# The first 512 rows of expert 0 moved into the attention, weight loads moved among the dispatches, and half tiles as two sums side by side

## The chip, the cores and the metric

The kernel runs on one core of a Trainium2 chip. The metric is the device time of one execution in microseconds (us); the kernel before takes 458.68 us (median of 6 runs, 457.5 to 460.51). A core has TensorE (matmuls, PE in the profile, its weight loads PEld), VectorE (DVE), ScalarE (ACT), GpSimd (POOL) and SyncE (SP). Each takes its instructions in order and waits on semaphores; transfers are issued from queues of GpSimd (software DMA), SyncE and ScalarE and run on 16 shared DMA engines.

## What is computed

A linear attention with phi(x) = elu(x) + 1, and on its result a mixture of experts with a noisy top-2 router:

```python
q_p, k_p = phi(q), phi(k)                       # (8 batches, 8 heads, 576, 64)
kv  = einsum('bhsd,bhse->bhde', k_p, v)
z   = sum(k_p, axis=2)
x   = einsum('bhsd,bhde->bhse', q_p, kv) / (einsum('bhsd,bhd->bhs', q_p, z)[..., None] + 1e-6)
x   = x.transpose(0, 2, 1, 3).reshape(4608, 512)

noisy = x @ w_gate + log1p(exp(x @ w_noise)) * noise      # 8 experts
top2  = the two largest of a row; top2_w = their softmax
for e in range(8):
    rows = the rows that have e among their two
    out[rows] += top2_w[rows, e] * (relu(x[rows] @ w1[e]) @ w2[e])   # w1 512x1024, w2 1024x512
```

## The kernel before

**Attention.** The 8 batches go in 4 groups of two. For each group: `load` brings q, k, v (GpSimd queue, cast to bf16), `exp` (ScalarE) and `phi` (VectorE) make phi(k) and phi(q), `kv_mm` multiplies phi(k) by v, `kv_ev` masks the result into `kvbd` (VectorE), `kv_b1` and `kv_b2` append the router's weights, already multiplied by kv, `qt` transposes phi(q), and `num` (three steps t per group; part 0 on TensorE, part 1 on VectorE) gives x (in `xr`, one of two buffers by turns) and the router's logits. `attention()` writes the order of all engines out by hand: group n's q and k are prepared beside group g = n - 1's `num` and routing.

**Routing.** Per unit (`UNITS`: groups 0, 1, 2 whole, group 3 in two parts) `rt_a` makes logits and noise scale, `rt_b` the top two and, with matmuls against a triangle of ones, each row's rank within its expert; `rt_c` adds the running count `carry` and so gets each row's position. `dispatch` scatters rows of x with an indirect DMA per column and choice into the DRAM table `x_sorted` (18 for a whole group, 72 in all), a short memset between two of them. Every row appears twice: as a first visit (kind F, the lower-numbered of its two experts) and a second (kind S). `ROUNDS` holds bounds: after the unit named, `carry` of experts 0, 1, 2 is raised to at least this row, so that rows below the bound are complete and may be read while later dispatches run.

**Experts.** A block is up to four tiles of 128 rows of one expert. `xn_load` brings its rows (SyncE queue), `meta_load` gates and indices, `xn_t` transposes on TensorE with a copy on ScalarE, `mm1` is relu(x @ w1) in eight parts (TensorE, then ScalarE), `mm2` is the product with w2 per tile, eight matmuls of 128x128 by 512 into one PSUM bank, then y = gate * sum on VectorE. First visits are put into the DRAM table `part` (SyncE). Second visits gather their first part (`gather`, GpSimd) into L, add it and scatter y to the output (`put`, GpSimd). Between F and S an expert has a mixed tile kind M: rows fetched by an indirect DMA (`mid_gather`, tile xm), two tiles, the second half full (64 rows). Experts 0 and 7 end with a half tile too. So there are eight half tiles: one of expert 0, one each of experts 1 to 6, one of expert 7, which is the last of all.

`interval(cur, prev, weights, nxt)` interleaves on TensorE: `mm1` of the current block, two parts at a time, with one `mm2` tile of the block before, and the transposes of the next block after the second and third of these. The gather of the next block and weight loads follow.

**The seam.** `routing()` runs after the attention: block a0 (expert 0, F tiles 0 to 3) with the ranks of units 3 and 4 between its parts, then a1 (expert 1, F 0 to 2), b0 (expert 0, F 4 and 5), b1 (expert 1, F 3 and 4), a2 (expert 2, F 0 to 3), c0 (expert 0, F 6 to 9, the last one half full). `xn_load(b0)`, b1 and a2 need the dispatches of unit 2; c0 needs all. `w_load(e, i)` is one of four weight pieces of an expert (512 KB in bf16): those of experts 0 and 1 stand among the dispatches of units 1 and 2, those of 2 and 3 after the last dispatch.

GpSimd's order from 64.8 us on, as the time line has it: 12 dispatches of unit 0, a q load, 6 more, unit 1 with four pieces, unit 2 with four pieces, unit 3 (12), unit 4 (6), the last dispatch written at 181.16, eight weight pieces, gathers of xm.

Lines named later: 261 `num`, 378 the memset between dispatches, 387 `dispatch`, 431 and 435 `w_load`, 443 `meta_load`, 498 `mid_gather`, 560 and 563 `xn_load`, 586 and 590 `xn_t`, 607 `gather`, 624 and 626 `mm1`, 635 to 641 `mm2`, 649 and 655 `put`. In the kernel after, the same code stands 1 to 34 lines lower.

Of the kernel before, what the change touches and what calls it, by code (L numbers as in the profile page):

```python
# [15 lines left out]
P = 128  # L16
# [17 lines left out]
ROUNDS = [(1, (512, 384, 256)), (2, (768, 640, 512))]  # L34
# [15 lines left out]
def build_constants(tc, consts, w_gate, w_noise, noise):  # L50
# [23 lines left out]
    c["gap"], c["gap2"] = tile_("gap", [P, 192]), tile_("gap2", [P, 352])  # L74
# [48 lines left out]
class PhaseA:  # L123
# [252 lines left out]
    def apart(self):  # L376

        self.nc.gpsimd.memset(self.c["gap"][:], 0.0)  # L378
# [22 lines left out]
class PhaseB:  # L401


    def __init__(self, ctx, tc, w1, w2, x_sorted, part, out):
# [5 lines left out]
        self.yp = [pool("B_y", 4)]  # L410
# [4 lines left out]
        self.left, self.ready = [], set()  # L415
# [212 lines left out]
    def mm2(self, b, t):  # L628
# [5 lines left out]
        for fc in range(8):  # L634
            nc.tensor.matmul(out=ps[0:m], lhsT=b["hT"][:, fc, t * P : t * P + m], rhs=w2[:, fc, :],  # L635
                             start=(fc == 0), stop=(fc == 7))
# [3 lines left out]
        else:  # L640
            nc.vector.tensor_scalar(out=y[0:m], in0=ps[0:m], scalar1=gate, scalar2=None, op0=ALU.mult)

    def put(self, b, t):
# [9 lines left out]
        if kind != "F":  # L653
# [6 lines left out]
            tc.add_to_no_dep_group("osc", r.ins)  # L660
            nc.gpsimd.memset(self.c["gap2"][:], 0.0)
# [82 lines left out]
def attention(pa, pb, c, x_sorted, zrow):  # L744
# [30 lines left out]
    first = pb.block(0, ("F", 0, 4))  # L775
    for g in range(3):
# [7 lines left out]
        if g == 1:  # L784
            pa.dispatch(0, 6, 9)
# [8 lines left out]
        pa.phi(n, "q", 0, 1)  # L794
        pa.num(g, 2, 1)
        pa.phi(n, "q", 2)
        if g == 0:
            pa.load(3, "k")
        pa.rt_a(g)
        pa.kv_ev(n, 0)  # L800
        pa.kv_ev(n, 1)
        pa.kv_b1(n)
        pa.qt(n, 0)
# [4 lines left out]
        if g == 0:  # L808
            pa.dispatch(0, 0, 6)
        else:  # L810
            pb.w_tiles(g - 1)
            for i in range(4):
                pa.dispatch(g, 2 * i, 2 * i + 2)
                pb.w_load(g - 1, i)
            pa.dispatch(g, 8, 9)
        if g == 1:
            pb.xn_load(first, 0)
            pb.meta_load(0, "F", 0, 4, 0)
            pb.meta_load(1, "F", 0, 3, 0)
# [4 lines left out]
    pa.num(3, 0, 1)  # L824
    pa.num(3, 1, 0)
# [4 lines left out]
    return first  # L830


def routing(pa, pb, c, first):

    pb.left += [0] * 6 + [1] * 5 + [2] * 4
# [3 lines left out]
    pb.xn_load(a1, 0)  # L839
    pb.meta_load(0, "F", 4, 2, 1)  # L840
    pb.xn_load(b0, 1)
    pb.meta_load(1, "F", 3, 2, 1)
    pb.xn_load(b1, 1)
    pb.meta_load(2, "F", 0, 4, 1)
    pb.xn_load(a2, 1)
    pb.xn_t(a0, 0)
    pb.xn_t(a0, 1)
    pb.mm1(a0, 0)
    pa.rt_b(3)
    pb.mm1(a0, 1, 2)  # L850
    pa.rt_c(3)
    pa.dispatch(3)
    pa.rt_a(4)
# [142 lines left out]
```

## Time and profile before

| what | value |
|---|---|
| median of 6 runs | 458.68 us |
| profiled execution | 460.76 us |
| its span, first to last instruction | 458.9 us |
| TensorE busy | 365.5 us (80%) |
| GpSimd busy | 286.9 us (63%) |
| ScalarE, VectorE busy | 192.9 us (42%), 179.2 us (39%) |
| mean granted TensorE clock | 0.903 |
| first dispatch, last dispatch (GpSimd) | 64.8 us, 181.16 us |
| last matmul ends, last scatter written, end | 449.8 us, 451.8 us, 458.9 us |

The profile is of one execution. Its lines of slices cut the span into 40 parts of 11.5 us; a digit is the busy share of an engine in tenths, in the row PEclk the granted TensorE clock in tenths. Lines of the time line read: start, length, engine, line, operation, out<-in, shapes, number of instructions merged, and in brackets the idle time of the engine before it with what ended it. "SPq" is SyncE's own instruction, the issue of a DMA. A group of instructions has: busy us, mean ns of one, idle time before and its releaser. Durations of matmuls are from first input to last output, so that successive ones overlap; the distance of their starts is what they cost.

### The profile page before, as it was taken

Reading aid. Unit: us, or ns where it says so; the run is one execution under the profiler, and the core shown is the slowest. Engines: PE = TensorE matmul, PEld = TensorE weight load, DVE = VectorE, ACT = ScalarE, POOL = GpSimd, SP = SyncE. Lnnn points to the kernel's source line nnn. Section 1 sums busy time; section 2 is a strip of 40 time slices with the busy share of each in tenths; the row PEclk is TensorE's granted clock in tenths of the full one; section 3 lists DMA queues with packets and bytes.
Section 4 is the critical chain, followed back from the end, with each engine's and each line's share of the span. In section 5 each row is a group of like instructions: output and inputs, shape, how many; then the busy total and the mean of one; then the engine's idle time right before and its main releaser. Section 6 shows DMA issues by size and latency. Waiting matters only on the chain.

```text
span 458.9 us, 7065 instructions
## 1 busy us (share of the span) xinstructions
PE 365.5 (80%) x2585; PEld 217.4 (47%) x2585; DVE 179.2 (39%) x481; ACT 192.9 (42%) x313; POOL 286.9 (63%) x425
## 2 busy tenths in 40 slices
PE   0195475654527777999999999999999999999992
PEld 0184364543423334644565544645545554554450
DVE  0836989899764502212232112131131131221131
ACT  1709564452305322554344543345335335445420
POOL 7130239898888889520036736549758876776883
PEclk9998767657656889999999999999999999999996
DMA  9999994656679774998446696995996996644541
GB/s 130 206 234 208 208 208 141 132 153 138 164 190 221 172 249 150 213 252 194 154 131 186 185 225 168 248 238 172 234 235 190 218 229 210 226 141 118 170 157 66
DMA packets 63234, 85.59 MB, mean 187 GB/s; under 512 B 16111, under 2 KB 45938, under 8 KB 63190
## 3 DMA queue, kind: packets, MB, share of 16 engines
q0 software_dynamic: 36416, 63.92, 62.1%
q1 hardware_dynamic: 25110, 20.96, 15.3%
q10 hardware_dynamic: 1664, 0.18, 0.5%
q8 instruction: 22, 0.36, 0.3%
q14 instruction: 22, 0.18, 0.1%
HBM read 83.88 MB, written 33.79 MB: 256 GB/s over the span
## 4 chain that ended last, share of the span: by engine, by line
PE 52%; POOL 15%; DMA 14%; issue 9%; DVE 4%; ACT 2%; SPq 1%; POOLq 0%; ACTq 0%; DVEq 0%
PE b L635 26%; PE b L624 23%; POOL x_sorted L387 9%; DMA kq<-in_q_dram 7%; PE t L586 3%; DMA xn<-x_sorted 3%; POOL gap L378 2%; DMA xm<-x_sorted,m_idx 2%; ACT e L169 2%; POOL L L607 1%; DMA x_sorted<-xr,posi 1%; DMA meta7S<-x_sorted 1%; POOL kq L154 1%; SPq L443 1%; POOL w L431 1%
## 5 line engine op out<-in xcount | busy, mean ns | idle before, releaser
L624 PE MATMUL b<-xt,w 128*128 128x512 bf16 (+5 forms) x800 | 150.8, 334 | 5.1 <-issue 2.9
L635 PE MATMUL b<-w,hT 128*128 128x512 bf16 (+1 forms) x640 | 151.6, 380 | 0.0
L626 ACT ACTIVATE hT<-b 128x512 bf16<-128x512 f32 (+5 forms) x200 | 97.2, 496 | 117.0 <-PE b L624 98.1
L624 PEld LDWEIGHTS <-w 128*128 128x128 bf16 x800 | 76.4, 99 | 63.1 <-issue 12.0
L635 PEld LDWEIGHTS <-hT 128*128 128x128 bf16 (+1 forms) x640 | 62.8, 99 | 68.3 <-issue 3.2
L387 POOL DMA_INDIRECT x_sorted<-xr,posi x72 | 74.6, 1036 | 21.1 <-issue 13.0
L590 ACT COPY xt<-t 128x1024 bf16<-128x1024 bf16 x32 | 32.4, 1012 | 57.2 <-PE t L586 48.6
L607 POOL DMA_INDIRECT L<-part,mgi x12 | 12.0, 1004 | 54.2 <-DMA xn<-x_sorted 37.6
L655 POOL DMA_INDIRECT out_dram<-y,si x34 | 33.9, 997 | 15.2 <-DVE y L639 9.8
L169 ACT ACTIVATE e<-kq 128x2304 bf16<-128x2304 bf16 x16 | 33.1, 2121 | 21.7 <-PE misc L198 9.6
L607 POOL DMA_INDIRECT L<-part,gi x34 | 34.7, 1021 | 9.3 <-issue 5.4
L198 PE MATMUL misc<-v,e 64*128 64x192 bf16 x144 | 20.4, 319 | 21.3 <-DVE e L179 21.3
L198 PEld LDWEIGHTS <-e 64*128 64x128 bf16 x288 | 22.0, 126 | 30.7 <-DVE e L179 29.0
L261 PE MATMUL num<-kvbd,pqt 128*64 128x162 bf16 x288 | 18.7, 303 | 13.0 <-DVE lwt L279 8.0
L198 PE MATMUL b<-v,e 64*128 64x192 bf16 x144 | 20.4, 319 | 7.0 <-DVE e L179 7.0
L586 PE MATMUL t<-ident,xn 128*128 128x128 bf16 (+1 forms) x256 | 20.9, 221 | 5.3 <-DMA xn<-x_sorted 3.9
L272 DVE TENSOR_TENSOR xr<-num,rden 128x384 bf16<-128x384 f32 x48 | 23.4, 550 | 2.4 <-DMA x_sorted<-xr,posi 2.1
L586 PEld LDWEIGHTS <-xn 128*128 128x128 bf16 (+1 forms) x256 | 17.2, 99 | 14.4 <-DMA xn<-x_sorted 5.3
L655 POOL DMA_INDIRECT out_dram<-y,msi x12 | 11.7, 979 | 17.9 <-DVE y L639 13.6
L261 PEld LDWEIGHTS <-pqt 128*64 128x64 bf16 x288 | 15.6, 149 | 15.3 <-issue 9.9
L639 DVE SCALAR_TENSOR_TENSOR y<-b,mgate,L 128x512 f32<-128x512 f32 (+1 forms) x12 | 9.0, 746 | 31.9 <-PE b L635 29.4
L179 DVE TENSOR_TENSOR e<-e,kq 128x2304 bf16<-128x2304 bf16 x16 | 21.2, 1354 | 0.3
(164 smaller groups left out, 361.5 us busy)
## 6 DMA issues: line engine op xcount, KB each, us to landing
w<-in_moe_w_dram POOLq DMA_DIRECT2D x32, 512.0 KB
part<-y SPq DMA_DIRECT2D x39, 256.0 KB
kq<-in_k_dram POOLq DMA_DIRECT2D x8, 576.0 KB
kq<-in_q_dram POOLq DMA_DIRECT2D x8, 576.0 KB
v<-in_v_dram POOLq DMA_DIRECT2D x8, 576.0 KB
xn<-x_sorted SPq DMA_DIRECT2D x11, 256.0 KB
xn<-x_sorted SPq DMA_DIRECT2D x6, 384.0 KB
xn<-x_sorted SPq DMA_DIRECT2D x4, 512.0 KB
```

The lines of the kernel that those rows point to most:

```text
L169: self.nc.scalar.activation(out=e, in_=x, func=ACT.Exp)
L198: nc.tensor.matmul(out=self.kvps[g, h, j][:, KVM * i : KVM * i + KVM], lhsT=e[half, hp, ci, :], rhs=v[half, hp::4, 64 * ci : 64 * ci + 64] ...
L261: nc.tensor.matmul(out=ps[half, hp, KVW * i : KVW * i + KVW], lhsT=self.pqt[g, 3 * t + i][:, hp, half], rhs=self.kvbd[g][:, j, hp, :], sta ...
L272: nc.vector.tensor_tensor(out=_ap(xr, [[ROW_W, 3], [256, 2], [1, 64]], off=3 * t * ROW_W + 64 * hp), in0=_ap(ps, [[KVW, 3], [64, 2], [1, 6 ...
L387: r = self.nc.gpsimd.indirect_dma_start(out=self.x_sorted, out_offset=bass.IndirectOffsetOnAxis(ap=self.r["posi", u][:, ci - c0, sl : sl + ...
L586: nc.tensor.transpose(ps[:, i, dc, 0:m], self.xn(b, t, dc), self.c["ident"][0:m, 0:m])
L590: nc.scalar.copy(out=b["xt"][:, :, t * P : t * P + 2 * P].rearrange("p c (i r) -> p i c r", i=2), in_=ps)
L607: r = nc.gpsimd.indirect_dma_start(out=L[0:m].bitcast(INT32), out_offset=None, in_=self.part.bitcast(INT32), in_offset=bass.IndirectOffset ...
L624: nc.tensor.matmul(out=ps[:, 0:n], lhsT=w1[:, dc, fc * P : fc * P + P], rhs=b["xt"][:, dc, 0:n], start=(dc == 0), stop=(dc == 3))
L626: nc.scalar.activation(out=b["hT"][:, fc, 0:n], in_=ps[:, 0:n], func=ACT.Relu)
L635: nc.tensor.matmul(out=ps[0:m], lhsT=b["hT"][:, fc, t * P : t * P + m], rhs=w2[:, fc, :], start=(fc == 0), stop=(fc == 7))
L655: r = nc.gpsimd.indirect_dma_start(out=self.out, out_offset=bass.IndirectOffsetOnAxis(ap=self.m[e, kind, i]["si"][0:m], axis=0), in_=y[0:m ...
```

## The change

Five edits. (1) Block a0 of four tiles becomes two blocks of two tiles, a0 and a1. Their loads, transposes, `mm1` and, for a0, `mm2` and `put` now stand in `attention()`, in the last group's turn and after it; `ROUNDS` gets a bound after unit 0 (256 rows of expert 0), so that a0 may be read once group 0 is dispatched, a1 once group 1 is; expert 2's bound after unit 1 goes. Within the last turn `kv_ev` moves ahead of the second `num` step. What was block a1 (expert 1) keeps its place in `routing()`, with the second half of the new a1 in front of it. (2) The weight pieces of expert 0 go among the last dispatches of unit 0, those of expert 1 among unit 1's, none among unit 2's, those of expert 2 into unit 3's; those of expert 3 follow the last dispatch. (3) In `mm2` a half tile (m = 64 rows) no longer takes eight matmuls into PSUM partitions 0 to 63: parts 0 to 3 of the hidden dimension are summed into partitions 0 to 63 and parts 4 to 7 into 64 to 127, by turns, and VectorE adds the second sum with one more instruction. (4) Buffers: y 3 + 6 in a rotation of three instead of 4 + 4, L 8 instead of 10, one tile for both memsets. (5) The memset after the very last scatter goes.

```diff
-ROUNDS = [(1, (512, 384, 256)), (2, (768, 640, 512))]
+ROUNDS = [(0, (256, 0, 0)), (1, (512, 384, 0)), (2, (768, 640, 512))]
...
     def mm2(self, b, t):
-        for fc in range(8):
-            nc.tensor.matmul(out=ps[0:m], lhsT=b["hT"][:, fc, t * P : t * P + m], rhs=w2[:, fc, :],
-                             start=(fc == 0), stop=(fc == 7))
+        n = P // m
+        for fc in range(8 // n):
+            for i in range(n):
+                f = fc + i * (8 // n)
+                nc.tensor.matmul(out=ps[i * m : i * m + m], lhsT=b["hT"][:, f, t * P : t * P + m], rhs=w2[:, f, :],
+                                 start=(fc == 0), stop=(fc == 8 // n - 1), skip_group_check=n > 1)
...
+        if n > 1:
+            nc.vector.scalar_tensor_tensor(out=y[0:m], in0=ps[m:P], scalar=gate, in1=y[0:m], op0=ALU.mult, op1=ALU.add)
...
 def attention(pa, pb, c, x_sorted, zrow):
-    first = pb.block(0, ("F", 0, 4))
+    a0, a1 = pb.block(0, ("F", 0, 2)), pb.block(0, ("F", 2, 2))
+    pb.w_tiles(0)
+    pb.w_tiles(1)
     for g in range(3):
...
         if g == 1:
-            pa.dispatch(0, 6, 9)
+            for i in range(3):
+                pa.dispatch(0, 6 + i, 7 + i)
+                pb.w_load(0, i)
+            pb.w_load(0, 3)
+            pb.xn_load(a0, 0)
+            pb.meta_load(0, "F", 0, 2, 0)
...
         pa.phi(n, "q", 0, 1)
+        if g == 2:
+            pa.kv_ev(n, 0)
+            pa.kv_ev(n, 1)
+            pb.xn_t(a0, 0)
         pa.num(g, 2, 1)
         pa.phi(n, "q", 2)
+        if g == 2:
+            pb.mm1(a0, 0, 1, 2, 3)
...
         pa.rt_a(g)
-        pa.kv_ev(n, 0)
-        pa.kv_ev(n, 1)
+        if g < 2:
+            pa.kv_ev(n, 0)
+            pa.kv_ev(n, 1)
         pa.kv_b1(n)
+        if g == 2:
+            pb.mm1(a0, 4, 5, 6, 7)
...
         if g == 0:
             pa.dispatch(0, 0, 6)
+        elif g == 1:
+            for i in range(4):
+                pa.dispatch(1, 2 * i, 2 * i + 2)
+                pb.w_load(1, i)
+            pa.dispatch(1, 8, 9)
+            pb.xn_load(a1, 1)
+            pb.meta_load(0, "F", 2, 2, 1)
+            pb.meta_load(1, "F", 0, 3, 1)
         else:
-            pb.w_tiles(g - 1)
-            for i in range(4):
-                pa.dispatch(g, 2 * i, 2 * i + 2)
-                pb.w_load(g - 1, i)
-            pa.dispatch(g, 8, 9)
+            pa.dispatch(2)
...
     pa.num(3, 0, 1)
+    pb.mm2(a0, 0)
+    pb.put(a0, 0)
     pa.num(3, 1, 0)
     pa.num(3, 1, 1)
     pa.num(3, 2, 0)
     pa.rt_a(3)
     pa.num(3, 2, 1)
+    pb.mm2(a0, 1)
+    pb.put(a0, 1)
+    pb.xn_t(a1, 0)
+    pb.mm1(a1, *range(8))
+    return a1
...
 def routing(pa, pb, c, first):
-    pb.xn_t(a0, 0)
-    pb.xn_t(a0, 1)
-    pb.mm1(a0, 0)
+    pb.xn_t(a1, 0)
     pa.rt_b(3)
-    pb.mm1(a0, 1, 2)
+    pb.mm2(a0, 0)
+    pb.put(a0, 0)
+    pb.xn_t(a1, 1)
     pa.rt_c(3)
-    pa.dispatch(3)
+    pa.dispatch(3, 0, 3)
+    pb.w_load(2, 0, 1)
+    pa.dispatch(3, 3, 6)
+    pb.w_load(2, 2, 3)
+    pb.mm2(a0, 1)
+    pb.put(a0, 1)
     pa.rt_a(4)
-    pb.mm1(a0, 3, 4, 5)
+    pb.mm1(a1, 0, 1, 2)
     pa.rt_b(4)
-    pb.mm1(a0, 6, 7)
+    pb.mm1(a1, 3, 4, 5)
     pa.rt_c(4)
+    pb.mm1(a1, 6, 7)
     pa.dispatch(4)
     pb.mids()
-    pb.w_tiles(2, 1)
-    pb.xn_t(a1, 0)
-    pb.xn_t(a1, 1)
-    pb.interval(a1, a0, (), b0)
-    pb.w_load(2, 0, 1, 2, 3)
+    pb.xn_t(b0, 0)
     pb.interval(b0, a1, (), b1)
```

In `routing()` after the change the names shift: its `a0` is the new a1 of the attention (rows 256 to 511 of expert 0), its `a1` is expert 1's block, called "block 1" in the prediction. Not shown: `pb.left` (the count of tiles yet to be put) is set at the start, the group numbers of early reads go up by one, the buffer pools are as said under (4), and `put` returns ahead of the memset for expert 7's last tile.

## The prediction

> **What bounds the kernel now.** I read the page first (busy shares, then the 40 slices), then the clock line of the cores, busy time by window, the time line of each engine from 60 to 215 us, SyncE's waits, and the groups with shapes kept apart.
>
> From about 165 us on TensorE is the bound; before that it is not. The windows (each engine's busy us, then clock and DMA) say so, and the slices show who is full earlier: GpSimd.
>
> ```profile
> PE   0195475654527777999999999999999999999992
> POOL 7130239898888889520036736549758876776883
> PEclk9998767657656889999999999999999999999996
> 165.00:202.00 37.00, 32.65 (x200) 18.84 (x200) 6.23 (x9) 13.70 (x28) 26.22 (x40) 0.95 0.88 217
> 202.00:450.00 248.00, 245.97 (x1468) 131.03 (x1468) 57.30 (x121) 108.76 (x204) 151.95 (x214) 1.00 0.73 193
> ```
>
> Two stages follow: up to 181 us GpSimd's dispatches, one after the other without a pause; from 202 us TensorE with 2 us of idle time in 248. What joins them decides this change. It is the load of the last four tiles of expert 0 (block c0), which needs every dispatch:
>
> ```profile
> 179.75 0.28 POOL L378 MEMSET gap<- 128x192 f32 x1
> 180.19 0.97 POOL L387 DMA_INDIRECT x_sorted<-xr,posi  x1 [0.17 <-issue]
> 181.36 1.52 POOL L431 DMA_DIRECT2D w<-in_moe_w_dram  x2
> 186.71 0.40 SPq L443 DMA_DIRECT2D meta4F<-x_sorted  x1
> 187.21 0.61 SPq L560 DMA_DIRECT2D xn<-x_sorted  x1
> 191.33 1.05 POOL L498 DMA_INDIRECT xm<-x_sorted,m_idx  x1 [1.84 <-DMA w<-in_moe_w_dram]
> 195.38 1.01 POOL L498 DMA_INDIRECT xm<-x_sorted,m_idx  x1 [2.58 <-DMA w<-in_moe_w_dram]
> 198.69 1.00 POOL L498 DMA_INDIRECT xm<-x_sorted,m_idx  x1 [1.90 <-DMA w<-in_moe_w_dram]
> 202.28 0.62 PE L586 MATMUL t<-ident,xn 128*128 128x128 bf16 x8 [0.63 <-DMA xn<-x_sorted]
> ```
>
> The reader is to see: the last dispatch is written at 181.16; 5.55 us later SyncE may issue (186.71); c0's rows leave at 187.21 and TensorE gets them only at 202.25, 15.0 us later. In front of them stand eight weight pieces (experts 2 and 3), issued from 181.36 on; the xm gathers, which wait for pieces two, three and four, date these at 191.3, 195.4 and 198.7, so a piece takes 3.3 to 4.1 us. TensorE arrived 0.63 us too early: c0 is a gate, with little slack on either side.
>
> An earlier gate is the load of b0 (rows 512 to 767 of expert 0), which needs the dispatches of group 2. TensorE was idle before it too, and ran slowly after it:
>
> ```profile
> 154.93 0.97 POOL L387 DMA_INDIRECT x_sorted<-xr,posi  x1 [0.17 <-issue]
> 162.35 0.47 SPq L560 DMA_DIRECT2D xn<-x_sorted  x1
> 165.46 1.03 PE L586 MATMUL t<-ident,xn 128*128 128x128 bf16 x8 [2.75 <-DMA xn<-x_sorted]
> 166.28 2.56 PE L624 MATMUL b<-xt,w 128*128 128x384 bf16 x8
> 170.41 1.46 PE L624 MATMUL b<-xt,w 128*128 128x384 bf16 x8
> ```
>
> For the half tiles, the rows that matter (busy us, mean ns):
>
> ```profile
> 36.62 1.04 PE L261 MATMUL num<-kvbd,pqt 128*64 128x162 bf16 x24
> L635 PE MATMUL b<-w,hT 128*64 128x512 bf16 x64 | 15.3, 382 | 0.0
> L639 DVE SCALAR_TENSOR_TENSOR y<-b,mgate,L 64x512 f32<-64x512 f32 x6 | 4.5, 743 | 12.9 <-PE b L635 12.9
> ```
>
> **What the Trainium skill says.** "TensorEngine Tiling (Array Packing)", section Theoretical Speedup: a stationary operand of at most 64 columns allows two tiles side by side, up to twice as fast. The trace agrees: the 24 products of line 261 alternate between the two halves and take 1.04 us, the last one's drain of 0.23 us included, so they start 35 ns apart; 162 columns alone take 68 ns (eight products of 512 columns take 1.73 us, 0.42 ns a column). "TensorE: Matmul & The Clock Gate", section What's actually happening: after an idle window the array runs at half clock for about 3.4 us. The trace agrees: after the 2.75 us gap above, eight 384-column products take 2.40 us from start to start instead of 1.30, the transposes 0.82 instead of 0.45, 1.5 us lost. "DMA: Bandwidth & Descriptors", section Queues, rings and completion order: each DMA engine takes the queues that have work in turns, by packets. The trace agrees loosely: c0's rows land before the eight pieces are through, but late.
>
> **The change, part by part.**
>
> *512 rows of expert 0 into the attention.* Off the stage after 140 us go 32x512 columns twice (64 x 0.216 = 13.8 us) and 16 transposes (0.9 us): 14.7 us of TensorE, with their ScalarE copies and relus and four y of 0.75 us. In the attention they fall beside VectorE, busy 18.4 of 20 us from 100 to 120, while TensorE has 13.0. Two waits are new there. xn_t(a0) stands in front of kv_b1, qt and the ranks of group 2; its rows need group 0's last dispatch, two weight pieces later than before (95.2 + 1.7 = 96.9), plus 5.5 and 3 us: 105.5, where TensorE ends kv_mm (105.46). With eight 256-column products at half clock I put the ranks of group 2 about 4 us later (116.0 to 120), positions at 124; dispatch(2) needs them at 132: hidden. xn_t(a1) waits for group 1's dispatches: these end 3.3 us later (four weight pieces among them, 0.84 us each: 2.24 us from dispatch to dispatch with a piece, 1.40 without), so at 130.4, the rows land near 140, a1's products end near 149, and the ranks of group 3 and mm2(a1), queued behind, give positions at 152 to 154. dispatch(3) needs them at 157: 3 to 5 us of cover. The put of a0 now stands on SyncE in front of block 1's load; its y follows VectorE's last attention step (138), so this load goes at 140, in time for the transposes at 149.
>
> *Weights among dispatches.* Before, eight pieces stood ahead of the last dispatch; now twelve: 4 x 0.84 = 3.3 us. Each software DMA also waits for the one eight before it (eight semaphores taken in turn). Four pieces and a q load within 13 us near 90 us (there the q load alone keeps the DMA 1.20 and 0.95 busy from 88 to 96) can make this bite: none to 3 us, I take 1.5. The last dispatch ends at 181.2 + 4.8 = 186.0.
>
> *The gates.* b0's position in the queue is the same (eight pieces ahead in both): rows at about 165. TensorE now stands empty before it from about 160. Then b0, b1, the first half of a2: 16 x 0.43 + 5 x 1.73 + 1.4 of transposes, + 4 x 0.865 + 2 x 1.73 = 23.9 us, with copies and the cold start 3 us: it is at c0's transposes by 192. c0's load goes at 186.0 + 5.55 + 0.5 = 192.0. Only four pieces (expert 3) stand before it, from about 188 on, 13 us: it lands between 198 (taking turns) and 203 (behind them). I take 201, against 202.25: -1.3. After 9 us idle TensorE starts cold: +1.5. So of 14.7 us moved away nothing is left: they are turned into idle time ahead of c0. c0 off the gate would show 14.7 in full.
>
> *From there.* The load for block (1, F5) went at 203.92 and came at 213.83, 0.49 us late; it now finds a free queue: -0.5.
>
> *Half tiles.* Eight of them (one in c0, one each in experts 1 to 6, one at the very end). Eight products become four pairs: 4 x 0.216 = 0.86 us each. VectorE pays 0.74 us more for each, in a stage where it is 23% busy (57.3 of 248): hidden, except on the last tile, where it takes back the gain but 0.1. Expert 5's is also lost: TensorE waits 1.05 us at 368.5 for xm of expert 6, whose chain (meta7S at 340.3, then GpSimd without pause) doesn't shrink. 6 x 0.86 + 0.1 = 5.3. Bounds: 0 (no overlap) to 6.9.
>
> *At nothing:* y buffers 8 to 9; L buffers 10 to 8 (two blocks hold at most 4 + 4, and a gather stands behind the puts of the block before); one gap tile; one max of 0.16 us per group; expert 2's bound; the last memset (0.41 us, beside the last DMA, which ends 7 us later).
>
> Sum: -1.3 + 1.5 - 0.5 - 5.3 = -5.6 us. The profiled execution took 460.76 (span 458.9), so it would be 455.2; it lies above the median, 458.68, from which the same step gives **453.1**.
>
> **Rivals.**
> - *The rows count.* c0 lands when TensorE comes, at 194 to 197 without long idle: for it, half as many pieces before it; against it, a load only 5 us later than before. 7 us more than above: **446**. In full: 458.7 - 14.7 - 5.3 = 438.7, which I hold for nearly excluded.
> - *The halves don't overlap.* For it: the pairs read a shared stream of 512 columns and no trace line has that; against it: line 261. 453.1 + 5.3 = **458.4**.
> - *Slower: ranks behind products.* TensorE works in order, so group 3's ranks wait for a1's rows, eight products and block 1's rows; every us of positions after 157 shifts dispatch(3), the end of the dispatches, c0 and the end. For it: mm1(a1) with two PSUM buffers and a cold clock; against it: the cover of 3 to 5 us. It decides from positions at 165 on; at 167, 10 us late, **463**. It would show as GpSimd waiting at the first dispatch of group 3.
>
> **The numbers.** My forecast 0.52 (own range 449.5 to 456.5), the rows count 0.20, halves without overlap 0.14, ranks late 0.14. Range 445 to 459. A measurement of this kernel tells about 0.5% (2.3 us) from no change: faster 0.70, same 0.17, slower 0.13.
>
> **What would show it.** Right: GpSimd without a wait before the dispatches of group 3, its last one near 186; TensorE idle 5 to 10 us before c0's transposes near 201; half tiles 0.87 us long; the end 5 to 6 us earlier. Wrong: TensorE full from 165 on (rows count), 1.73 us half tiles, or a wait of VectorE at a y or of GpSimd for positions.

## The result, and the profile after

The changed kernel takes 461.00 us, median of 19 runs (457.99 to 467.30), the kernel before 458.86 us on the same chip (median of 40 runs, 457.24 to 460.51): ratio 1.0044, 95% interval 1.0029 to 1.0059. The run of 467.30 was in a slower state, which the ratios leave out; without it the highest is 464.21. Two later series, on other chips, gave 1.0019 [1.0000, 1.0038] and 1.0036 [1.0014, 1.0058]. That is no change by the 0.5% of the prediction, on the slow side of it; the forecast was 453.1 in a range of 445 to 459.

The profiled execution took 458.04 us (span 456.2). It lies 3 us *below* the median of its kernel; the profiled execution of before (460.76) lay 1.9 us *above* its own. What the two traces show, -2.7 us, is therefore not what the medians show, +2.1.

The page of the changed kernel, its slices, and the same two windows as before (busy us of TensorE, weight loads, VectorE, ScalarE, GpSimd, then clock and DMA):

```profile
PE   0194576553854969939999999999999989999990
PEclk9998756577877679979999999999999999999997
165.00:202.00 37.00, 29.99 (x187) 17.43 (x184) 8.77 (x39) 14.37 (x29) 29.25 (x44) 0.92 1.04 220
202.00:450.00 248.00, 240.47 (x1468) 128.44 (x1468) 63.41 (x127) 108.94 (x204) 153.54 (x215) 0.99 0.70 190
```

From 165 to 202 us TensorE has 29.99 us of work instead of 32.65, at a lower clock, and the slices have a hole (a 3) at 194 to 205 us, where before there were nines. The time line of GpSimd, SyncE and TensorE around it:

```profile
159.28 0.97 POOL L388 DMA_INDIRECT x_sorted<-xr,posi  x1 [3.91 <-issue]
186.74 0.97 POOL L388 DMA_INDIRECT x_sorted<-xr,posi  x1 [0.17 <-issue]
192.31 0.63 SPq L562 DMA_DIRECT2D xn<-x_sorted  x1
203.82 1.03 PE L588 MATMUL t<-ident,xn 128*128 128x128 bf16 x8 [7.28 <-DMA xn<-x_sorted]
```

The chain of waits names the same place (start, length, what):

```profile
186.74 4.91 DMA x_sorted<-xr,posi
192.31 11.47 DMA xn<-x_sorted
204.86 2.87 PE b L626 x8
```

The last dispatch leaves at 186.74, its bytes and SyncE's turn take until 192.31, and c0's rows need 11.5 us more; TensorE stands idle for 7.28 us and then runs its first eight products in 2.87 us instead of 1.73.

What the DMA engines did in these 11.5 us can be read from the packets of each queue: q0 is GpSimd's (here mostly the weight pieces of expert 3), q1 is SyncE's. Each line gives packets, MB and the time that they took as a share of the 16 engines' time. The windows are 192.3 to 195.6 us (first line), 195.6 to 199.2 (next two) and 199.2 to 202.8 (last two):

```profile
q0 software_dynamic: 268, 0.52, 101.1%
q0 software_dynamic: 601, 0.71, 112.8%
q1 hardware_dynamic: 497, 0.02, 19.5%
q0 software_dynamic: 454, 0.46, 74.5%
q1 hardware_dynamic: 459, 0.41, 43.5%
```

For 3.3 us no packet of SyncE's queue moves. Then its packets and those of GpSimd's queue move at about the same rate. But c0's rows, 448 packets of 1 KB, come second: in front of them on SyncE's queue stands `meta4F`, issued 0.5 us earlier (8 KB, 16 bytes for each of 512 rows), and it takes as long as the rows.

The half tiles do what they should (group, then one of them in the time line):

```profile
L641 PE MATMUL b<-w,hT 128*64 128x512 bf16 x64 | 8.4, 385 | 0.0
L649 DVE SCALAR_TENSOR_TENSOR y<-b,mgate,y 64x512 f32<-64x512 f32 x6 | 4.5, 752 | 0.2
...
232.78 1.05 PE L641 MATMUL b<-w,hT 128*64 128x512 bf16 x8
233.77 1.26 PE L626 MATMUL b<-xt,w 128*128 128x320 bf16 x8
```

Eight half products start 0.99 us before the next work (before: 1.73 us); together they take 8.4 us instead of 15.3.

So there are two terms, and every run below is read by them: when c0's first transpose starts, and how long it is from there to the end of the span (the tail). In this pair c0 moved from 202.28 to 203.82 (+1.5) and the rest went from 256.6 to 252.4 (-4.2).

### The profile page after: what moved, and what is told of

Read it like the earlier page. It is cut to its first block, busy times and chain, and to the rows that moved or that the text cites. A ratio compares the mean times of both kernels' runs of the same rounds, so it can differ in the third digit from the quotient of the medians.

```text
span 456.2 us, 7145 instructions
## 1 busy us (share of the span) xinstructions
PE 362.4 (79%) x2617; PEld 217.1 (48%) x2617; DVE 185.1 (41%) x493; ACT 194.2 (43%) x321; POOL 286.7 (63%) x424
## 4 chain that ended last, share of the span: by engine, by line
PE 60%; POOL 16%; DVE 8%; DMA 8%; issue 4%; ACT 1%; another core or an unknown queue 1%; ACTq 0%; POOLq 0%; SPq 0%; DVEq 0%
PE b L626 25%; PE b L641 25%; POOL x_sorted L388 11%; PE t L588 4%; POOL gap L379 3%; DMA xn<-x_sorted 3%; DMA xm<-x_sorted,m_idx 2%; DVE xr L273 2%; DMA wst<-in_moe_w_noise_dram 2%; DMA x_sorted<-xr,posi 2%; DVE e L180 1%; PE misc L199 1%; PE num L262 1%; PE b L199 1%; POOL w L433 1%
## 5 line engine op out<-in xcount | busy, mean ns | idle before, releaser
L626 PE MATMUL b<-xt,w 128*128 128x256 bf16 (+5 forms) x832 | 154.9, 333 | 9.5 <-ACT xt L592 3.9
L641 PE MATMUL b<-w,hT 128*128 128x512 bf16 (+1 forms) x640 | 147.4, 385 | 0.1
L628 ACT ACTIVATE hT<-b 128x256 bf16<-128x256 f32 (+5 forms) x208 | 98.4, 484 | 110.6 <-PE b L626 99.0
L626 PEld LDWEIGHTS <-w 128*128 128x128 bf16 x832 | 81.4, 101 | 67.9 <-issue 18.1
L641 PEld LDWEIGHTS <-hT 128*128 128x128 bf16 (+1 forms) x640 | 59.6, 100 | 66.0 <-issue 5.6
L592 ACT COPY xt<-t 128x1024 bf16<-128x1024 bf16 x30 | 30.4, 1012 | 52.7 <-PE t L588 47.5
L647 DVE TENSOR_SCALAR y<-b,meta2F 128x512 f32<-128x512 f32 x14 | 10.5, 749 | 40.1 <-PE b L641 40.1
L379 POOL MEMSET gap<- 128x192 f32 x72 | 21.0, 291 | 0.0
```

The costliest lines, as they stand in the source:

```text
L379: self.nc.gpsimd.memset(self.c["gap"], 0.0)
L626: nc.tensor.matmul(out=ps[:, 0:n], lhsT=w1[:, dc, fc * P : fc * P + P], rhs=b["xt"][:, dc, 0:n], start=(dc == 0), stop=(dc == 3))
L628: nc.scalar.activation(out=b["hT"][:, fc, 0:n], in_=ps[:, 0:n], func=ACT.Relu)
L641: nc.tensor.matmul(out=ps[i * m : i * m + m], lhsT=b["hT"][:, f, t * P : t * P + m], rhs=w2[:, f, :], start=(fc == 0), stop=(fc == 8 // n ...
```

## Experiments

The later runs were on three chips, here called 2, 5 and 11. On chip 5 and in the first two traces there are waits of 1 to 4.5 us, mostly of ScalarE, that nothing in the profile explains ("remote", "issue"); on chips 2 and 11 there are almost none. Times are compared by their ratio to the kernel before on the same chip.

| run | chip | median us | ratio [95%] | last dispatch | c0's load issued | idle before c0 | c0 starts | c0 to end |
|---|---|---|---|---|---|---|---|---|
| before (first) | first | 458.86 | 1 | 180.19 | 187.21 | 0.63 | 202.28 | 256.6 |
| e5 before | 5 | 458.70 | 1.0007 [0.9986, 1.0028] | 180.23 | 184.85 | 0 | 199.68 | 256.8 |
| e17 before | 5 | 459.24 | 1.0000 [0.9983, 1.0016] | 180.95 | 186.47 | 0 | 200.75 | 257.0 |
| change (first) | first | 461.00 | 1.0044 [1.0029, 1.0059] | 186.74 | 192.31 | 7.28 | 203.82 | 252.4 |
| e1 change | 11 | 457.06 | 1.0019 [1.0000, 1.0038] | 183.76 | 189.69 | 13.09 | 202.08 | 253.0 |
| e13 change | 2 | 456.86 | 1.0036 [1.0014, 1.0058] | 184.47 | 188.96 | 10.57 | 200.33 | 254.0 |
| e2 half tiles alone | 11 | 449.47 | 0.9879 [0.9847, 0.9910] | 179.65 | 182.73 | 0 | 195.33 | 251.3 |
| e9 half tiles alone | 5 | 453.63 | 0.9872 [0.9842, 0.9902] | 180.91 | 185.63 | 0 | 202.04 | 250.6 |
| e10 change, no half tiles | 5 | 464.91 | 1.0115 [1.0086, 1.0143] | 188.07 | 194.15 | 7.21 | 205.17 | 259.1 |
| e8 half tiles, w(2) among | 5 | 456.78 | 0.9957 [0.9928, 0.9986] | 184.27 | 189.29 | 5.59 | 201.07 | 255.0 |
| e7 change, w(2) after | 5 | 458.63 | 0.9983 [0.9962, 1.0005] | 184.44 | 189.27 | 0 | 205.51 | 251.1 |
| e3 change, w(3) late | 11 | 450.73 | 0.9875 [0.9843, 0.9907] | 183.64 | 189.08 | 3.61 | 192.92 | 256.5 |
| e6 change, w(3) after xm | 5 | 456.57 | 0.9941 [0.9919, 0.9963] | 187.30 | 193.00 | 0 | 197.07 | 258.4 |
| e15 change, w(3) held | 2 | 446.40 | 0.9809 [0.9782, 0.9836] | 184.37 | 188.44 | 3.72 | 192.17 | 253.0 |
| e18 change, w(3) held | 5 | 450.69 | 0.9821 [0.9798, 0.9844] | 188.00 | 192.54 | 0 | 197.86 | 251.0 |
| e16 both orders undone | 2 | 451.77 | 0.9933 [0.9910, 0.9956] | 179.37 | 182.45 | 0 | 197.74 | 253.1 |
| e12 half tiles, w(3) held | 5 | 453.58 | 0.9876 [0.9845, 0.9908] | 180.38 | 187.03 | 0 | 201.31 | 250.4 |
| e4 ranks first | 11 | 457.64 | 1.0029 [1.0005, 1.0054] | 185.41 | 189.15 | 10.49 | 201.93 | 255.1 |
| e14 ranks first | 2 | 456.46 | 1.0023 [1.0000, 1.0045] | 182.84 | 187.97 | 8.93 | 200.02 | 252.3 |
| e11 ranks first, w(3) held | 5 | 458.63 | 0.9953 [0.9931, 0.9974] | 184.41 | 191.84 | 0 | 206.20 | 251.9 |

"w(2)" and "w(3)" are the four weight pieces of experts 2 and 3. The places in the table are of one profiled execution each, the medians of all runs.

**The same kernels again** (e1, e13, e5, e17; no edit). They give further traces of both kernels, since the first two executions lay on opposite sides of their medians:

> The changed kernel once more, for a second trace of it: the first profiled execution (458.04 us) lay 3 us under the median of its runs (461.0). Theory A (the seam: what is late is group 3's positions and with them the last dispatch, and expert 0's last four tiles, c0, land behind expert 3's weights): the trace shows GpSimd waiting 4 us or more at the first dispatch of group 3, c0's first transpose at 204 to 208 with TensorE idle 5 us or more before it, and from there to the end the same 252.4 us as in the first trace; the ratio to before is 1.003 to 1.006. Rival B (TensorE's later stage is where the runs differ): c0's transposes at 203.8 again, and the stretch from there to the end longer by the 3 us.

> The changed kernel a third time, as the reference on the same chip for the next three, and for a trace. Theory C: ratio 1.001 to 1.006; c0's load issued at 189 to 194, landed 11 to 13 us later, TensorE idle 5 to 13 us before it. If the chip is one of the slower ones, GpSimd waits near 4 us at group 3's first dispatch.

> The kernel before once more, for a second trace of it: the one the prediction rests on (span 458.9) is among the slowest of its runs, and the half-tile kernel, the same up to c0, reached c0 at 195.33 without a wait. Theory C (before, c0 isn't a gate: its load is issued near 183 and lands about when TensorE arrives): load issued 182 to 184, c0's transposes at 195 to 198 with under 1 us of idle, span 451 to 454. Rival (the first trace is typical): load issued at 187, transposes at 201 to 203.

> The kernel before a third time, for its trace. Theory C: TensorE, not c0's rows, sets the time at c0: first transpose at 195 to 197 on a chip without the unexplained waits, at 199 to 202 on one with them, in both cases with at most 0.7 us of idle before it; 256.5 to 257 us from there to the end. Rival (c0's rows are the gate of before): idle of 1 us or more before c0's transposes.

The changed kernel always waits for c0's rows: 7.28, 13.09, 10.57 us. On chips 2 and 11 GpSimd doesn't wait at group 3's first dispatch (e1: 154.84, 0.17 us), and the kernel is no better for it. c0 came at 202.08, a little earlier than in the first trace and not later, as theory A had it; the tail was 0.6 us longer. In both new traces of before TensorE finds c0's rows there; in e17 a wait of ScalarE 20 us earlier, which nothing explains, makes it late (time line of e17):

```profile
180.15 0.38 ACT L626 ACTIVATE hT<-b 128x256 bf16<-128x256 f32 x1 [3.94 <-remote]
...
199.02 1.89 PE L635 MATMUL b<-w,hT 128*128 128x512 bf16 x8
200.75 0.61 PE L586 MATMUL t<-ident,xn 128*128 128x128 bf16 x8
```

No idle time stands in the brackets of the last line. The rival of e17 (rows as the gate before) falls; the places that e5's theory gave are too early for chip 5 (load at 184.85 and not 182 to 184, c0 at 199.68 and not 195 to 198).

**Half tiles alone, and the change without them** (e2, e9, e10):

```diff
-        for fc in range(8):
-            nc.tensor.matmul(out=ps[0:m], lhsT=..., start=(fc == 0), stop=(fc == 7))
+        n = P // m
+        for fc in range(8 // n):
+            for i in range(n):
+                ...
```

> The kernel before with the half tiles of the change alone. Theory A: eight half tiles save about 0.75 us each by the changed kernel's trace (0.99 us from start to start in place of 1.73), less what the last one's second VectorE instruction takes, and less what stands before xm of expert 6: -4 to -5.5 us, ratio 0.988 to 0.991. Rival (a half tile's gain is taken up by later waits): within 1 us of before.

> The kernel before with half tiles alone once more, on the same chip as the next three, since the first run of it came from a chip on which all kernels took 3 us less and showed none of the unexplained waits of 1 to 4 us ('issue', 'remote') that the traces from the other chip have. Theory C: ratio 0.987 to 0.990 here too, and c0's transposes without a wait (under 1 us). Rival (the gain came from that chip): ratio above 0.994, as in the run with expert 2's pieces among the dispatches.

> The changed kernel with half tiles as eight products in a row again, all else as in the change. Theory C (half tiles pay everywhere, the rest of the change costs): 4.5 to 6 us slower than the changed kernel, ratio to before 1.012 to 1.018. Rival (half tiles and the rest aren't additive, as TensorE waits for xm later): ratio 1.006 to 1.010.

On two chips alike half tiles alone save 6.0 and 5.9 us, more than expected; in the traces the gain lies after c0 (251.3 and 250.6 us from there instead of 256.6 to 257.0). The change without half tiles is 5.3 us slower than before, just under what was expected: all that isn't half tiles, taken together, costs time. In e2 TensorE goes from a2 into c0 without a gap, since the load is issued 7 us earlier than in e1 on the same chip:

```profile
182.73 0.65 SPq L560 DMA_DIRECT2D xn<-x_sorted  x1
...
193.61 1.89 PE L638 MATMUL b<-w,hT 128*128 128x512 bf16 x8
195.33 0.61 PE L586 MATMUL t<-ident,xn 128*128 128x128 bf16 x8
```

On chip 11, the change (e1) thus has c0 6.75 us later than half tiles alone (202.08 against 195.33), although TensorE is free for it 6.3 us earlier: it waits 13.09 us for the rows, so from 188.99 on.

**Expert 2's pieces among the dispatches** (e8: added to half tiles alone; e7: taken out of the change):

```diff
+    pb.w_tiles(2, 1)
-    pa.dispatch(3)
+    pa.dispatch(3, 0, 3)
+    pb.w_load(2, 0, 1)
+    pa.dispatch(3, 3, 6)
+    pb.w_load(2, 2, 3)
...
-    pb.w_load(2, 0, 1, 2, 3)
```

> The kernel before with half tiles, and expert 2's four pieces among unit 3's dispatches as in the change; no row moved. Theory C: the last dispatch ends 3.4 us later than in the half-tile kernel (184.0), c0's load is issued at 188 to 190 instead of 182.7 and lands at 199 to 202, TensorE idle 4 to 7 us before it where the half-tile kernel had none: 5 to 7 us slower than that one, ratio to before 1.000 to 1.004, as slow as the whole change. Rival (it is the rows put into the attention that cost): ratio 0.988 again.

> The changed kernel with expert 2's four pieces behind the last dispatch, as before, and expert 3's behind these. Theory C (four more pieces ahead of the last dispatch, and their bytes under way beside it, make c0's load late): the last dispatch ends at about 181.3 instead of 184.7, c0's load is issued near 183 instead of 189.7 and lands near 195 instead of 202; TensorE waits for expert 2's weights at a2 (about 186 to 190). 4 to 6 us less than the changed kernel, ratio to before 0.988 to 0.993. Rival (the last dispatch isn't what makes the load late): load issued within 2 us of 189.7, time unchanged.

The time line of e8:

```profile
184.27 0.97 POOL L387 DMA_INDIRECT x_sorted<-xr,posi  x1 [0.17 <-issue]
...
189.29 0.67 SPq L560 DMA_DIRECT2D xn<-x_sorted  x1
...
193.58 1.89 PE L638 MATMUL b<-w,hT 128*128 128x512 bf16 x8
201.07 1.04 PE L586 MATMUL t<-ident,xn 128*128 128x128 bf16 x8 [5.59 <-DMA xn<-x_sorted]
```

Last dispatch, load and wait come as theory C said, with no row moved: 5.59 us of idle that half tiles alone don't have, and 3.9 us of time (0.9957 less 0.9872, of 459; from two series on the same chip). Expected were 5 to 7. The two traces don't show the loss where theory C has it: c0 starts no later in e8 than in e9 (201.07 against 202.04, since TensorE comes late for c0 by itself in e9), and the tail is 4.4 us longer. Of these, 2.1 are the slow start after the idle time (from c0's first transposes to the next ones 4.24 us instead of 2.17); the rest wasn't traced. So e8 shows that these four pieces alone make the load late and cost time, but not the whole way from the one to the other. e7 tells less: GpSimd waited 3.95 us at group 3's first dispatch, so the last one came at 184.44, not 181.3; c0's rows weren't waited for, but TensorE came as late as 205.51, after unexplained waits and behind ScalarE:

```profile
175.32 1.86 PE L626 MATMUL b<-xt,w 128*128 128x256 bf16 x8 [3.22 <-ACT xt L592]
187.88 2.46 PE L626 MATMUL b<-xt,w 128*128 128x256 bf16 x12 [2.45 <-ACT hT L628]
```

**Expert 3's pieces in front of c0's rows** (e3: to the second and third block after c0; e6: into c0's interval; e15, e18: there, but held until the rows of (1, F5) have landed; e12: the same hold on half tiles alone):

```diff
-    pb.w_load(3, 0, 1, 2, 3)
...
+            if i == 0:
+                nc.gpsimd.tensor_copy(out=c["gap2"][:, 0:1], in_=nxt["xn"][:, 1, 0:1])
+                parts += [(3, k) for k in range(4)]
             pb.interval(b, prev, parts, nxt)
```

(The hold is shown. e6 has no copy; e3 has two pieces each at i = 1 and i = 2, and no copy.)

> The changed kernel with expert 3's four weight pieces moved from behind the last dispatch to the second and third block after c0. Theory A: c0's rows have nothing in front of them and land about 196 instead of 203.8; TensorE, which arrives at 196.5, waits little and isn't cold: 7.5 to 9 us less than the changed kernel, some 452 us, ratio to before about 0.985. Rival (c0's rows are slow for another reason, the dispatches just before them): the load still takes 10 us or more, gain under 2 us. Rival (the pieces are late where they stand now): c0 early, but a wait of TensorE at expert 3's first products or at xm.

> The changed kernel with expert 3's four pieces right after the xm gathers of experts 1 and 2 (in the interval of c0) in place of before c0's rows. Theory C: c0 lands about 193 as in the run with the pieces at the second and third block; the two waits for xm there (1.87 and 2.18 us, late since the pieces stood in front of the gathers) become smaller; the load of (1, F5) may come up to 2 us late. 446 to 448 us of span, ratio to before 0.979 to 0.985, better than the kernel before with half tiles alone (0.988). Rival (these pieces cost TensorE the same wherever they stand): 0.9875 again.

> The changed kernel with expert 3's pieces held until the rows of (1, F5) have landed, and nothing else. Theory C: c0's rows land 3 to 4 us after their issue, so at 193 to 197; no wait at (1, F5) (it was 4.73 us with the pieces in front of it); about 251.5 to 253 us from c0 to the end: 445 to 450 us of span, ratio to before 0.977 to 0.986, faster than half tiles alone. Rival (ranks first was not what made the run with both changes slow, holding the pieces was): ratio 0.993 or more.

> The changed kernel with expert 3's pieces held until the rows of (1, F5) have landed, again. On a chip without the unexplained waits: ratio 0.979 to 0.984, as in the first run. On one with them: TensorE comes to c0 at 196 to 199 instead of 190, so the rows are there or nearly; 447 to 452 us of span, ratio 0.978 to 0.988. If it is the hold that made the run with ranks first slow, 0.992 or more.

> The kernel before with half tiles and with expert 3's pieces held until the rows of (1, F5) have landed; no row moved, expert 2's pieces as before. Theory C (before, TensorE and not c0's rows set the time at c0): c0's transposes no earlier than in the half-tile kernel; only the wait at (1, F5) goes (1.83 us there): 0 to 2.5 us faster than the half-tile kernel, ratio 0.983 to 0.989. Then the move of rows is worth at most what the run before this one gains over it. Rival (c0's rows were the gate before, as the prediction had it): 4 us or more faster than the half-tile kernel.

The time line of e15:

```profile
184.37 0.97 POOL L388 DMA_INDIRECT x_sorted<-xr,posi  x1 [0.17 <-issue]
...
188.44 0.46 SPq L562 DMA_DIRECT2D xn<-x_sorted  x1
...
192.17 1.04 PE L588 MATMUL t<-ident,xn 128*128 128x128 bf16 x8 [3.72 <-DMA xn<-x_sorted]
...
198.97 0.18 POOL L996 CAST gap<-xn 128x1 f32<-128x1 bf16 x1 [7.02 <-DMA xn<-x_sorted]
199.42 1.57 POOL L433 DMA_DIRECT2D w<-in_moe_w_dram  x2 [0.27 <-issue]
```

With nothing in front, c0's rows take 3.73 us from issue to TensorE (3.84 in e3) instead of 11.37 in e13 on the same chip. The packets say how: only nine packets of GpSimd's queue move among SyncE's, the first of SyncE's moves 0.5 us after the issue, and those of `meta4F` and the rows are through 2.9 us after it, against 10.5 us in e13. Against e13, c0 starts 8.2 us earlier and the tail is 1.0 us shorter: the spans differ by 9.1, the medians by 10.5. The result holds on chip 5 (e18). This one edit makes the change faster than both kernels, 0.981 and 0.982.

Where the pieces go instead matters. In e3 they stand in front of xm gathers, in e6 in front of the load for (1, F5); the time lines of e3 (first two) and e6:

```profile
289.77 0.40 PE L588 MATMUL t<-ident,xm 128*128 128x128 bf16 x4 [1.87 <-DMA xm<-x_sorted,m_idx]
359.92 0.40 PE L588 MATMUL t<-ident,xm 128*128 128x128 bf16 x4 [2.18 <-DMA xm<-x_sorted,m_idx]
```

```profile
212.90 1.04 PE L588 MATMUL t<-ident,xn 128*128 128x128 bf16 x8 [4.73 <-DMA xn<-x_sorted]
```

Both tails are 256 to 258 us: what c0 gained was partly given back at the next load in the queue. e6 thus missed its expectation, and e3 fell short of its own (0.9875 for 0.985), with the waits for xm that its second rival named. e12 is the cross test: the same hold does nothing for half tiles alone (0.9876 after 0.9872), and c0 comes at 201.31, without a wait, as before. Taking pieces away from c0's rows pays only where TensorE is early for them.

**Both weight orders undone** (e16: the edit of e7 and the hold). It asks whether the moved rows cost anything by themselves:

> The changed kernel with expert 2's pieces behind the last dispatch, as before, and expert 3's held as in the run before this: rows moved and halves kept, both weight orders undone. If the moved rows cost nothing: the last dispatch ends 3.4 us earlier than in the changed kernel, c0's rows are there when TensorE comes, and the ratio is 0.977 to 0.988. Rival (the moved rows themselves cost 4 us, in TensorE's order around group 3's ranks): ratio 0.992 to 0.998, with TensorE at c0 as late as 203 to 206 without waiting for rows.

Its time line:

```profile
179.37 0.97 POOL L388 DMA_INDIRECT x_sorted<-xr,posi  x1 [0.17 <-issue]
...
186.02 0.77 PE L626 MATMUL b<-xt,w 128*128 128x512 bf16 x2 [2.14 <-DMA w<-in_moe_w_dram]
189.43 2.74 PE L626 MATMUL b<-xt,w 128*128 128x512 bf16 x6 [2.64 <-DMA w<-in_moe_w_dram]
...
197.74 0.61 PE L588 MATMUL t<-ident,xn 128*128 128x128 bf16 x8
```

The last dispatch is 5 us earlier than in e13, more than the 3.4 expected, but now a2 waits for expert 2's weights, 2.14 and 2.64 us. The ratio, 0.9933, is the rival's, its mechanism is neither's: with the rows moved, TensorE is at a2 by 184, and w(2) must come early for it. Beside e15 (0.9809) this says that w(2) among the dispatches belongs to the move and pays, once w(3) is out of c0's way.

**Group 3's ranks first** (e4, e14; e11 with the hold):

```diff
-    pb.xn_t(a1, 0)
-    pb.mm1(a1, *range(8))
     return a1
...
+    pb.xn_t(a0, 0)
+    pb.mm1(a0, 0, 1)
     pa.rt_b(3)
+    pa.rt_c(3)
+    pb.mm1(a0, 2, 3, 4, 5, 6, 7)
```

(In `routing()` the names are a0 for the second 256-row block and a1 for expert 1's first block.)

> The changed kernel with group 3's ranks and positions in front of six of the eight hidden parts of a1, so that they don't stand behind a1's products. Theory A: positions at about 146 instead of 158.5, GpSimd doesn't wait at the first dispatch of group 3 (3.9 us in the trace), the last dispatch ends near 184 instead of 187.7, c0 lands about 4 us earlier (200), and the time is 3.5 to 4.5 us less than the changed kernel's, about 457; if the varying part of its time is here too, its runs spread less. Rival (GpSimd's queue is the bound there anyway, by its dispatches and lanes): last dispatch within 1 us of 187.7, no gain.

> The changed kernel with group 3's ranks in front of six of a1's eight hidden parts, again, for a slower chip. If the late positions make part of the loss: GpSimd doesn't wait at group 3's first dispatch, c0 lands up to 4 us earlier than in the changed kernel beside it, and the time is 2 to 4 us less. Rival (the unexplained waits of ScalarE and TensorE in a1's products only move behind the ranks, TensorE comes later to b0, b1 and a2, and SyncE's stores in front of c0's load with it): c0's load issued within 1.5 us of the changed kernel's, time within 1.5 us. On a chip without these waits: no difference, as in the first run of it.

> The changed kernel with group 3's ranks in front of six of the eight hidden parts of a1, and with expert 3's pieces held on GpSimd until the rows of (1, F5) have landed (a copy of one column of these rows). Theory C: no wait of GpSimd at group 3's first dispatch, last dispatch near 184, c0's load at 188 to 189 and landed at 192 to 193, TensorE idle 3 us before it, no wait at (1, F5): span 446 to 449, ratio to before 0.972 to 0.982. Rival (the late pieces hold up experts 2 and 3): c0 as early, but waits for xm or for weights of 2 us or more, ratio 0.985 or more.

e4 and e14 gain nothing (1.0029 and 1.0023 beside 1.0019 and 1.0036). Both met chips on which the positions are in time anyway, so the case they were for, a late group 3 with the rest of the change as it is, was not tried. e14 adds one thing: its last dispatch is 1.6 us earlier than e13's, its load 1.0, and c0 starts at 200.02 instead of 200.33: c0's rows land no earlier for it. e11 ran on chip 5: GpSimd no longer waits and the last dispatch comes at 184.41, and yet c0 starts at 206.20, without a wait for rows. The time line of ScalarE shows where TensorE loses time:

```profile
149.47 0.38 ACT L628 ACTIVATE hT<-b 128x256 bf16<-128x256 f32 x1 [4.47 <-remote]
153.03 0.38 ACT L628 ACTIVATE hT<-b 128x256 bf16<-128x256 f32 x1 [3.17 <-remote]
160.16 0.38 ACT L628 ACTIVATE hT<-b 128x256 bf16<-128x256 f32 x1 [3.15 <-remote]
164.45 1.01 ACT L592 COPY xt<-t 128x1024 bf16<-128x1024 bf16 x1 [2.46 <-remote]
```

These 13.3 us lie inside a1's products and behind them; e18, the same without ranks first on the same chip, had no such wait over 2 us there and is 6 us faster (0.9821 against 0.9953). Whether ranks first brings these waits about isn't shown; e4 and e14 have the same order without them. e11's expectation of 0.972 to 0.982 was missed, and not by the rival's cause.

## Why the prediction was wrong, and where right

*Half tiles, -5.3: right in size, by another sum.* Alone they give -5.9 and -6.0. One tile saves 0.74 us, not 0.86 (four pairs take 0.99 us, not 0.86), and eight times 0.74 is 5.9: hardly anything was lost elsewhere. The wait before expert 6's xm, which was to take one tile's gain, is 1.05 to 1.55 us in the three traces of before, 0.45 in e2, 1.73 in e9 and 1.60 in the change: it grows by at most 0.7 us, and not clearly.

*The tail: the sum right, its terms by luck.* Slow start +1.5, (1, F5) -0.5 and half tiles -5.3 make -4.3; the profiled pair shows -4.2. But without half tiles the tail is 2.2 us longer than before on the same chip (e10 against e5 and e17), not 1.0, where the wait before expert 6's xm has grown to 2.35 us; and half tiles alone shorten it by 6.3 us (e9), not 5.3.

*The issue of c0's load: the number right, by luck.* Forecast were 186.0 for the end of the last dispatch and 192.0 for the load; the trace has 187.71 and 192.31. The 5.55 us put between dispatch and load were read from the first trace of before, and there SyncE didn't wait for the dispatch:

```profile
179.45 0.38 ACT L626 ACTIVATE hT<-b 128x256 bf16<-128x256 f32 x1 [3.90 <-remote]
186.07 0.33 SPq L649 DMA_DIRECT2D part<-y  x1
```

SyncE stores y of an earlier block until 186.40 and then goes on to c0's loads (186.71); that y is late since TensorE and ScalarE are, after one of the unexplained waits. e5 and e17 have the stores in front of the load in the same way. Where SyncE does wait for the dispatch, 1.6 us (e2) to 4.5 us (e1) pass after it, and 4.1 in the first trace of the change: a dispatch 1.7 us later than forecast and a wait 1.4 us shorter cancel.

*c0's gate, "-1.3": the step that failed.* In the profiled pair c0 comes 1.5 us later and not 1.3 earlier. In the medians all that isn't half tiles, which was to give -1.3 + 1.5 - 0.5 = -0.3 us, costs 5.3 us on chip 5 (e10 against before) and 7.6 on chip 11 (e1 against e2, which is the kernel before up to c0). Three things were wrong.

- *The landing.* It was put 6 to 11 us after the issue, and 9 were taken, because four weight pieces stand in front and not eight. All five traces of the change and of ranks first, and e8 and e10, have 11.0 to 12.8. The number of pieces isn't what counts: with eight pieces (e2) the last of c0's packets moves 11.3 us after the issue, with four (first trace of the change) after 10.4. The prediction took from the Trainium skill that the DMA engines take the queues in turns, by packets ("DMA: Bandwidth & Descriptors", section Queues, rings and completion order), and the trace agrees, with 454 packets against 459. But then each of SyncE's packets, and `meta4F` has more of them than the rows, goes in turn with about one of the weights', for as long as there are any; and 3.3 us pass before the first. Why these pass isn't known. The same section says that a DMA's completion is signalled only after every earlier write of that DMA engine, across its queues; that isn't what made the rows late, as TensorE starts 1.1 us after their last packet (0.8 in e15).
- *The reference.* 202.25 is the landing in one execution of before, with the load held up as shown above. In the other traces of that kernel c0 starts at 199.68 and 200.75, and half tiles alone start it at 195.33 on a chip without the unexplained waits, all without idle time. So before, TensorE and not the rows set the time there, with the landing shortly before it (in e2 at 194.9 at the latest).
- *The work moved away.* "Off the stage after 140 us go" 14.7 us counts all four tiles, but the second two, a1, are worked on from 138 to 158 us, as the prediction itself places them; its first transposes and its last products in the changed kernel:

```profile
138.42 0.78 PE L588 MATMUL b<-ident,xt 128*128 128x128 bf16 x8
156.28 1.89 PE L641 MATMUL b<-w,hT 128*128 128x512 bf16 x8
```

So only half leaves the stage, and at c0 TensorE is 6.3 us earlier than with half tiles alone (e1 against e2, on one chip), about that half, and not 14.7. "c0 off the gate would show 14.7 in full" could not come true.

*"It lies above the median, from which the same step gives": also wrong.* A step against a near tie of one execution need not carry over to the medians. Between the profiled executions the error is 2.9 us (-2.7 for -5.6); the other 4.8 us up to +2.1 are where the two executions lie among their runs. Why the runs of the change spread over 6 us (without the one of 467.30), those of before over 3, was not traced.

*"Nothing is left" of the work moved away: right, and the reason is shown.* e15 and e18 differ from the change by expert 3's pieces alone. Even then the moved rows are worth only what these runs gain over half tiles alone: 2.3 us on chip 5 (0.9821 against 0.9872), some 3 us with e15 on chip 2 against e2 on chip 11. In e15 the last dispatch still gates c0, with 3.72 us of idle; in e18 c0 doesn't wait, and TensorE comes as late as 197.86 by itself.

*Cover of 3 to 5 us for group 3's positions: wrong on chip 5 and the first chip, held on the others.* The rival "ranks behind products" happened in its mild form: waits of 3.78 to 3.95 us at group 3's first dispatch (first trace, e6, e7, e10, e18). It isn't the cause of the loss: e1 and e13 have no such wait, and e18 has it and is faster than before. The rival "the rows count" was wrong for the change; with expert 3's pieces held, c0 comes in time for it (192.17 and 197.86), but the ratio is 0.981 and not the 0.972 that its 446 us stand for. "The halves don't overlap" is out.

## What to carry to other kernels

Before a stage is emptied to reach a gate earlier, move the gate: the same change that brought TensorE to c0 6.3 us earlier pushed the gated load 7 us back (e1 against e2), and four weight pieces that are first used at 265 us stood in front of it. Put bulk loads behind the load that an engine will wait for, with an explicit wait if the queue's order doesn't give it, and look at which load comes next before placing them (e3, e6). Count the packets of a load and not only its bytes, those of small loads ahead of it on its queue too: here 8 KB of `meta4F` took as long as the rows. Issuing the rows first would be the next thing to try; no run did. And take a gate's time from several executions: one trace can show a near tie as a gate.

## What was not expected of the hardware

- The same kernel before takes 455.0 and 455.5 us on two chips and 458.7 to 459.6 on a third, and the third has waits of ScalarE of 1 to 4.5 us without a releaser in the profile. They lie elsewhere from run to run (at 180 us in e17, at 145 to 165 in e11), and they can be longer than what an edit gains. The Trainium skill, "Runtime: NRT & Kernel Launch", section Instruction fetch mechanics, says that engines fetch their instructions in blocks by a DMA queue of their own, mostly hidden. The traces speak against such fetches as the cause: e11 has five of these waits from 145 to 165 us and one packet of the instruction queues there, at 163 us, and e1 has as many such packets in all and no such wait. The cause stays open.
- The sum in two halves side by side takes 0.99 us for four pairs of 512 columns, 14% above the 0.86 us of half the products.
- 448 rows of c0 (448 KB), behind 8 KB of `meta4F`, reach TensorE 3.7 to 3.8 us after their issue (e15, e3), or 11 to 13 us with four 512 KB weight pieces issued shortly before; with them, about one packet of each queue moves in turn, whatever its size (497 packets of 0.02 MB beside 601 of 0.71).
- After idle times of 2.4 to 2.8 us TensorE started slow in three traces (before, e8, e17: eight transposes in 1.03 to 1.04 us), after 2.85 us in e4 it didn't (0.62). So the length of the idle time alone doesn't decide it.
